# A fused attention and two dense layers: q and k turned by VectorE, reciprocal sums spread by DMA, one threshold per block, two rotating PSUM banks

## The chip, the cores and the metric

The kernel runs on one core of a Trainium2 chip. The metric is the device time of one execution in microseconds (us), as the median of several runs. TensorE (PE in the profile, PEld for its weight loads), VectorE (DVE), ScalarE (ACT) and GpSimd (POOL) have one instruction queue each and work through it in order. SyncE (SP) has the queue from which nearly all DMAs of this kernel are issued.

## The reference

```python
q, k, v: [4, 8, 576, 64]; tau: 0.02; moe_w_in, moe2_w_in: [512, 2048]; moe_w_out, moe2_w_out: [2048, 512]

scores = (1 / 8) * q @ k^T                          # per batch and head, 576 x 576
scores = where(scores >= max(scores, -1) - tau, scores, -1e9)
attn = exp(scores - max(scores, -1)); attn = attn / (sum(attn, -1) + 1e-9)
x = (attn @ v), heads side by side                  # 2304 tokens x 512
h = x @ moe_w_in;  g = where(h >= 1, h, where(h <= -1, 0, (h + 1)^2 / 4));  x = g @ moe_w_out
h = x @ moe2_w_in; g = h * clip(h + 3, 0, 6) / 6;                          out = g @ moe2_w_out
```

All inputs and the output are float32.

## The kernel before

**Jobs and blocks.** Attention is cut into 16 jobs, one for each batch and pair of heads, and a job into five blocks of query rows (four of 128 rows for both heads, and one that holds the 64 remaining rows of both heads). A step of the loop in `attention()` emits the score products of one block and the later stages of earlier blocks. For a block: `em_scores` multiplies `qt` and `kt` (both with the head's 64 dimensions on the partitions) into a pair of PSUM banks P0/P1 (L296); VectorE copies the negated scores to SBUF and takes their extreme (L309); `em_exp` runs the exponential on ScalarE (L320) and adds tau to the extreme on VectorE (L322, once for each of the block's two halves); `em_mask` masks and sums on VectorE (L328); `em_pt` and `em_tail` turn the masked block with TensorE against the identity (`turn`, L254) and ScalarE copies the result to SBUF (L352, L366); `pv_chunk` multiplies with v (L388), and ScalarE copies the result to `xu` (L394).

**q and k.** Both are loaded with rows on the partitions (`load_q`, `load_k`), and `unit_q` and `unit_k` turn them with five and six TensorE transposes (L254, tiles `qn` and `kn`) into a P pair, which ScalarE copies to `qt` (L266, scaling q) and `kt` (L277). The unit of job j+1 is emitted in the last steps of job j.

**The sums.** `pre_norm` takes the reciprocals of a job's nine columns of sums; GpSimd spreads each over 64 columns (L412). Some steps later `em_norm` turns them with TensorE (four transposes at L426 and one at L429, into a P pair) and VectorE multiplies `xu` by the result (L431, L437), after which `xu` is written to DRAM (`xd`, L434, L438).

**The first dense layer runs along.** After the fourth job (j = 3) is finished (`ready(0)`), `mode["mlp"]` is set. From then on each `yield` of `attention()` lets 0.57 units of the first dense layer (`dense1`: `em_h`, L633, and `em_part`, L695, over 256 token columns) be emitted into the same queues, and the weights are split into two parts by ScalarE, VectorE and GpSimd (`split_a`, `split_b`: L116 to L139). What is left of that layer after attention is emitted at once, and then the wide dense layers follow (`dense`: L633 and L675).

**PSUM banks.** While the dense layer runs along, all turns of masked blocks go to bank Q0, the product with v to Q1, `em_h` to Q2, and `em_part` accumulates in Q3. P0 and P1 are shared by the scores, the units and the norm.

**Order.** `attention()` has three branches for a step: one before `mode["mlp"]`, one for steps under 35, and one for later steps. A scheduler with a timeline model puts the emitted instructions in order on each engine, within the order that priorities and added dependencies (`after`) allow.

Of the kernel before, what the change touches and what calls it, by code (L numbers as in the profile page):

```python
# [18 lines left out]
def kernel(  # L19
# [27 lines left out]
    NW = len(WIDE)  # L47
    NF1 = 10
    MLAG = 2
    RAW = 3  # L50
# [145 lines left out]
    def zcol(x, c):  # L196
        return 8 if c == NBLK - 1 else c // 2 * 4 + x * 2 + c % 2

    jobs = [(b, hp) for b in range(NB) for hp in range(HP)]
    NJ = len(jobs)  # L200

    att_es = ExitStack()
# [5 lines left out]
    vn = [ap.tile([128, 5, 2, D], F32, name=f"vn{i}") for i in range(2)]  # L208
    qt, kt = {}, {}

    def rows(src):
        return src[0:MAIN, :].rearrange("(p c) d -> p c d", c=4)

    def load_q(j):
        if j >= NJ:
            return
        E = nc.sync if j else nc.scalar
        b, hp = jobs[j]
        for h in HEADS:
            src = q[b, 2 * hp + h]  # L220
            E.dma_start(out=qn[:, 0:4, h * D:(h + 1) * D], in_=rows(src))
            E.dma_start(out=qn[0:TAIL, 4, h * D:(h + 1) * D], in_=src[MAIN:SEQ, :])

    def load_k(j):
        if j >= NJ:
            return
        b, hp = jobs[j]
        for h in HEADS:
            src = k[b, 2 * hp + h]
            nc.sync.dma_start(out=kn[:, 0:4, h * D:(h + 1) * D], in_=rows(src))  # L230
            for r in range(2):
                nc.sync.dma_start(out=kn[r * TAIL:(r + 1) * TAIL, 4, h * D:(h + 1) * D], in_=src[MAIN:SEQ, :])

    def load_v(j):
        if j >= NJ:
            return
        b, hp = jobs[j]
        t = vn[j % 2]
        for h in HEADS:
            src = v[b, 2 * hp + h]  # L240
            nc.sync.dma_start(out=t[:, 0:4, h, :], in_=rows(src))
            nc.sync.dma_start(out=t[h * TAIL:(h + 1) * TAIL, 4, h, :], in_=src[MAIN:SEQ, :])
# [15 lines left out]
    def unit_q(j):  # L258
        if j >= NJ or j in qt:
            return  # L260
        tm = unit_bank().rearrange("p e n -> p (e n)")
        for c in range(5):
            turn(tm[:, c * 128:(c + 1) * 128], qn[:, c, :], c == 0)
        load_q(j + 1)
        qt[j] = ap.tile([128, SEQ], F32, tag="qt", name="qt", bufs=2)
        reads(S.activation(out=qt[j], in_=tm[:, 0:SEQ], func=ACTF.Copy, scale=taus[:, 1:2]))  # L266

    def unit_k(j):

        if j >= NJ or j in kt:  # L270
            return
        tm = unit_bank().rearrange("p e n -> p (e n)")
        for i, c in enumerate((4, 0, 1, 2, 3, 4)):
            turn(tm[:, i * 128:(i + 1) * 128], kn[:, c, :], i == 0)
        load_k(j + 1)
        kt[j] = ap.tile([128, SEQ + TAIL], F32, tag="kt", name="kt", bufs=2)
        reads(S.activation(out=kt[j], in_=tm[:, 128 - TAIL:128 + MAIN + TAIL], func=ACTF.Copy))  # L277
# [37 lines left out]
    def em_exp(j, i, x):  # L315
        p, nm, th, es = blk[j, i]
        if x >= (1 if i == NBLK - 1 else 2):
# [14 lines left out]
    def turned(j, g):  # L332
# [6 lines left out]
        return gt[g, j]  # L339

    def em_pt(j, i, h):

# [15 lines left out]
    def em_tail(j, i):  # L358
# [3 lines left out]
        t = turned(j, g)[1]  # L362
        tl = bank("Q0" if mode["mlp"] else "Q3")
        if i < NBLK - 1:
# [10 lines left out]
    def pv_chunk():  # L375
# [26 lines left out]
    def pre_norm(j):  # L402
        if j not in zt:
            return
        z = zt.pop(j)
        rz = ap.tile([128, 9, 1], F32, tag="rz", name="rz", bufs=2)
        V.tensor_scalar(out=z, in0=z, scalar1=1e-9, scalar2=None, op0=ALU.add)
        V.reciprocal(out=rz[:, :, 0], in_=z)
        rb = ap.tile([128, 4, 2, 64], F32, tag="rb", name="rb")
        for h in HEADS:  # L410
            src = rz[:, 0:8, :].rearrange("p (g h c) o -> p h g c o", g=2, h=2)[:, h]
            G.tensor_scalar(out=rb[:, :, h, :].rearrange("p (g c) n -> p g c n", g=2),  # L412
                            in0=src.to_broadcast([128, 2, 2, 64]),
                            scalar1=1.0, scalar2=0.0, op0=ALU.mult, op1=ALU.add)
        rbs[j] = (rz, rb)

    def em_norm(j):
# [4 lines left out]
        b, hp = jobs[j]  # L422
        rz, rb = rbs.pop(j)
        bm = unit_bank().rearrange("p e n -> p (e n)")
        for c in range(4):
# [16 lines left out]
    def attention():  # L442
# [35 lines left out]
        for t in range(n + 6):  # L478
            mode["t"] += 1
            mode["step"] = True  # L480
            if not mode["mlp"]:
# [9 lines left out]
                for x in now_at("z"):  # L491
                    pre_norm(*x)
                yield
                now = due(1)
# [18 lines left out]
                for x in now_at("n"):  # L513
                    em_norm(*x)
                    yield
            elif t < 35:
                if t < n:
                    em_scores(*order[t])
                    maskq.append(order[t])
                for x in now_at("z"):  # L520
                    pre_norm(*x)
                if t < n:
                    em_exp(*order[t], 0)
                    em_exp(*order[t], 1)
                masked()
                tails(2)
                for x in now_at("q"):
                    unit_q(*x)
                    yield
                for x in now_at("n"):  # L530
                    em_norm(*x)
                    yield
                pv_run(1)
                yield
                now = due(1)
                for x in now_at("k"):
                    unit_k(*x)
                    yield
                for b in now:
                    em_pt(*b, 0)  # L540
                    yield
                pv_run(2)
                for b in now:
                    if b[1] < NBLK - 1:
                        em_pt(*b, 1)
                        yield
                yield
                for b in now:
                    if b[1] in AFTER:
                        pvq.extend((b[0], AFTER[b[1]], c) for c in range(5))  # L550
            else:
# [5 lines left out]
                for x in now_at("z"):  # L557
                    pre_norm(*x)
                masked()
                yield  # L560
# [167 lines left out]
    def fin_out(g, a, i):  # L728
# [7 lines left out]
        if c < nmain:  # L736
            b, r = divmod(c, MAIN // 128)
            nc.sync.dma_start(out=out[b * SEQ:b * SEQ + MAIN, :].rearrange("(p c) d -> c p d", c=4)[r], in_=ob)
        else:
# [265 lines left out]
```

## Time and profile before

| | before |
|---|---|
| three runs, us | 1137.9, 1138.17, 1138.59; median 1138.17 |
| span of the profiled execution, us | 1136.9 (1.27 below the median of the runs) |
| TensorE busy | 1108.0 us, 97% of the span |
| ScalarE busy | 632.6 us, 56% |
| VectorE busy | 575.6 us, 51% |
| GpSimd busy | 404.3 us, 36% |

The span runs from the first to the last instruction of one profiled execution; a run's time also has what lies around it. "Busy" of TensorE is from modelled ends of pipelined matmuls, so two matmuls that overlap are both shown with their whole length: what a matmul takes from the engine is read from the distance of two starts, not from its length. Times in the rows are from the span's start, in us.

### The profile page before, as it was taken

What the parts mean: (1) busy time and instruction counts of PE and PEld (TensorE: products, weight loads), DVE (VectorE), ACT (ScalarE), POOL (GpSimd) and SP (SyncE); (2) the same over time, 40 slices, a digit from 0 to 9 for tenths busy, and PEclk for the clock granted to TensorE, in tenths of its full rate; (3) what the DMA queues carried; (4) which work ended last, traced back from release to release, by engine and by line L of the source; (5) the groups of instructions that cost most, each with busy time, mean ns of one, the idle gap of its engine ahead of it and who ended that gap; (6) DMA issues with size and microseconds to landing.
All of it is one profiled execution on the core that took longest, in us unless ns stands there. A gap on an engine that the chain in (4) does not pass through costs nothing.

```text
span 1136.9 us, 18024 instructions
## 1 busy us (share of the span) xinstructions
PE 1108.0 (97%) x6680; PEld 901.2 (79%) x6680; DVE 575.6 (51%) x1272; ACT 632.6 (56%) x1239; POOL 404.3 (36%) x383
## 2 busy tenths in 40 slices
PE   7998899999999999999999999999999999999998
PEld 5665567778777788788889988888888888898886
DVE  5888887766565565445545756557511111121111
ACT  5787987866666666556566766645432222333222
POOL 0222676411111111136645765557622222222221
PEclk8999999999999999999999999999999999999999
DMA  6434335222111210015322344533110110010001
GB/s 161 106 77 102 109 108 151 63 81 71 47 49 32 53 43 13 11 34 167 98 75 93 117 143 150 184 111 111 38 42 1 32 38 1 10 38 1 19 1 38
DMA packets 105368, 80.09 MB, mean 70 GB/s; under 512 B 66368, under 2 KB 90176, under 8 KB 105280
## 3 DMA queue, kind: packets, MB, share of 16 engines
q1 hardware_dynamic: 103920, 78.64, 23.9%
q8 instruction: 53, 0.87, 0.3%
q10 hardware_dynamic: 1360, 0.30, 0.1%
q14 instruction: 35, 0.29, 0.1%
HBM read 61.60 MB, written 17.30 MB: 69 GB/s over the span
## 4 chain that ended last, share of the span: by engine, by line
PE 88%; ACT 4%; DVE 4%; issue 1%; DMA 1%; POOL 1%; ACTq 0%; SPq 0%; DVEq 0%
PE Q L633 34%; PE P L675 27%; PE Q L695 7%; PE P L296 7%; PE Q L388 6%; PE Q L254 5%; DVE p L309 2%; ACT e L320 1%; PE P L254 1%; DVE p L328 1%; ACT Gf L352 1%; PE P L426 0%; POOL w_c L135 0%; DMA w_raw<-in_moe_w_in_dram 0%; DVE xl L617 0%
## 5 line engine op out<-in xcount | busy, mean ns | idle before, releaser
L651 POOL TENSOR_TENSOR gl<-r,gh 128x512 fp32r<-128x512 f32 (+1 forms) x190 | 203.3, 1071 | 548.4 <-ACT gh L650 547.9
L633 PE MATMUL Q<-xh,wih 128*128 128x512 f32 (+1 forms) x760 | 263.2, 346 | 2.5 <-DVE r L644 2.5
L633 PE MATMUL Q<-xh,wil 128*128 128x512 f32 (+1 forms) x760 | 257.0, 338 | 0.0
L633 PE MATMUL Q<-xl,wih 128*128 128x512 f32 (+1 forms) x760 | 256.8, 338 | 0.0
L647 DVE SCALAR_TENSOR_TENSOR r<-r,Q 128x512 f32<-128x512 f32 (+1 forms) x80 | 50.7, 634 | 249.0 <-ACT r L646 248.9
L650 ACT ACTIVATE gh<-r 128x512 fp32r<-128x512 f32 (+1 forms) x190 | 99.8, 526 | 126.2 <-PE P L675 53.3
L633 PEld LDWEIGHTS Q<-xh,wih 128*128 128x128 f32 x760 | 143.9, 189 | 25.0 <-issue 4.8
L633 PEld LDWEIGHTS Q<-xl,wih 128*128 128x128 f32 x760 | 143.9, 189 | 15.7
L633 PEld LDWEIGHTS Q<-xh,wil 128*128 128x128 f32 x760 | 143.8, 189 | 15.2
L646 ACT ACTIVATE r<-Q,three 128x512 f32<-128x512 f32 (+1 forms) x80 | 51.4, 643 | 143.7 <-PE Q L633 140.6
L309 DVE TENSOR_SCALAR_CACHE_REDUCE p<-P 128x576 f32<-128x576 f32 x144 | 104.3, 754 | 50.2 <-PE Q L254 32.0
L328 DVE SCALAR_TENSOR_TENSOR p<-p,th,e 128x576 f32<-128x576 f32 x144 | 121.3, 860 | 15.7 <-ACT e L320 14.9
L644 DVE SCALAR_TENSOR_TENSOR r<-r,Q 128x256 f32<-128x256 f32 (+1 forms) x110 | 55.0, 500 | 135.1 <-ACT r L643 127.7
L320 ACT ACTIVATE e<-p,nm 128x576 f32<-128x576 f32 x144 | 109.1, 774 | 25.4 <-DVE p L309 24.3
L254 PE MATMUL Q<-ident,p 128*128 128x128 f32 x656 | 109.8, 283 | 11.3 <-ACT Gf L352 4.9
L675 PE MATMUL P<-woh,gh 128*128 128x512 f32 x288 | 112.0, 390 | 0.6 <-DVE ob L733 0.6
L675 PE MATMUL P<-wol,gh 128*128 128x512 f32 x288 | 112.3, 390 | 0.0
L254 PEld LDWEIGHTS Q<-ident,p 128*128 128x128 f32 x656 | 74.5, 141 | 46.3 <-ACT Gf L352 12.7
L675 PE MATMUL P<-woh,gl 128*128 128x512 f32 x288 | 111.0, 390 | 0.0
L296 PE MATMUL P<-kt,qt 64*128 64x288 f32 (+1 forms) x640 | 100.5, 433 | 6.0 <-DVE p L309 4.9
L135 POOL TENSOR_TENSOR w_c<-w_c,w_raw 128x512 int32<-128x512 int32 x64 | 88.6, 1384 | 39.1 <-DVE w_c L133 22.7
L352 ACT ACTIVATE Gf<-Q 128x512 f32<-128x512 f32 x128 | 74.9, 594 | 40.0 <-PE Q L254 39.2
(84 smaller groups left out, 1865.1 us busy)
## 6 DMA issues: line engine op xcount, KB each, us to landing
w_raw<-in_moe_w_in_dram SPq DMA_DIRECT2D x32, 512.0 KB, 4.1
w_raw<-in_moe_w_out_dram SPq DMA_DIRECT2D x32, 512.0 KB, 3.7
kn<-in_k_dram SPq DMA_DIRECT2D x32, 128.0 KB, 2.6
vn<-in_v_dram SPq DMA_DIRECT2D x32, 128.0 KB, 2.9
x2p<-ob SPq DMA_DIRECT2D x16, 256.0 KB, 2.2
x2d<-ob SPq DMA_DIRECT2D x16, 256.0 KB, 4.1
xst<-x2d SPq DMA_DIRECT2D x16, 256.0 KB, 3.3
out_dram<-ob SPq DMA_DIRECT2D x16, 256.0 KB, 2.2
```

The source lines that it names most:

```text
L135: x = G.tensor_tensor(out=c.bitcast(I32), in0=c.bitcast(I32), in1=r, op=ALU.add)
L254: x = T.transpose(out, in_, ident)
L296: mm = T.matmul(o, qt[j][r, c], kt[j][r, k0:k0 + HS], start=True, stop=True, skip_group_check=True)
L309: reads(V.tensor_scalar(out=p[:, x], in0=s[:, :, 0:HS], scalar1=-1.0, scalar2=3e38, op0=ALU.mult, op1=ALU.min, accum_out=nm[:, x:x + 1]), ...
L320: pins["S"] = S.activation(out=e, in_=p[:, x], func=ACTF.Exp, bias=nm[:, x:x + 1], scale=-1.0)
L328: V.scalar_tensor_tensor(out=p[:, x], in0=p[:, x], scalar=th[:, x:x + 1], in1=e, op0=ALU.is_le, op1=ALU.mult, accum_out=zt[j][:, z:z + 1])
L352: S.activation(out=f[:, h, :, d0:d0 + 128], in_=tm.rearrange("p (c n) -> p c n", c=4), func=ACTF.Copy)
L633: mm = T.matmul(h, l[:, kk * 128:(kk + 1) * 128], r, start=(x == 0), stop=(x == 3 * KD - 1))
L650: x = S.activation(out=gh, in_=r, func=ACTF.Copy)
L651: y = G.tensor_tensor(out=gl, in0=r, in1=f32(gh), op=ALU.subtract)
L675: T.matmul(a, l, r, start=(first and x == 0), stop=(last and x == 2))
L695: mm = T.matmul(o, l, r, start=(f == fs[0] and x == 0 and i == 0), stop=(f == fs[-1] and x == 2 and i == 1), skip_group_check=True)
```

## The change

From job five (j = 4; `j >= JT`, 12 of 16 jobs) q and k are loaded in strips, in such a way that each 32x32 square already stands on the partitions where its transpose belongs; one VectorE transpose, which turns 32x32 squares, makes `qt` and `kt`, and GpSimd scales q. In 14 of 16 jobs (`OVER`: all but the fourth and the last) the reciprocals are turned by VectorE as one 128x32 tile, written to DRAM as nine rows, read back one step later with each row repeated on 64 partitions (`fetch_norm`), and GpSimd multiplies `xu` by them. The threshold is one VectorE instruction for both halves of a block. While the dense layer runs along, turns and products with v take two banks in turn (`rotate`). The branch for steps under 35 is gone. From the second batch on, rows of q, k and v are loaded, and rows of the output stored, in natural order.

```diff
+    NAT = 1
+    JT = 4
...
     def zcol(x, c):
-        return 8 if c == NBLK - 1 else c // 2 * 4 + x * 2 + c % 2
+        return 8 if c == NBLK - 1 else x * 4 + c
...
+    OVER = [j for j in range(NJ - 1) if j != HP - 1]
...
+    def strips(t, s0, src, h):
+        n = src.shape[0] // 32
+        flat = t.rearrange("p c n -> p (c n)")
+        for x in range(2):
+            p0 = 64 * h + 32 * x
+            nc.sync.dma_start(out=flat[p0:p0 + 32, 32 * s0:32 * (s0 + n)].rearrange("p (s d) -> p s d", d=32),
+                              in_=src[:, 32 * x:32 * x + 32].rearrange("(s p) d -> p s d", p=32))
...
     def load_q(j):
...
-            E.dma_start(out=qn[:, 0:4, h * D:(h + 1) * D], in_=rows(src))
+            if j >= JT:
+                strips(qn, 0, src, h)
+                continue
+            E.dma_start(out=qn[:, 0:4, h * D:(h + 1) * D], in_=rows(src, b))
...
     def load_k(j):
...
-            nc.sync.dma_start(out=kn[:, 0:4, h * D:(h + 1) * D], in_=rows(src))
+            if j >= JT:
+                strips(kn, 2, src, h)
+                strips(kn, 0, src[MAIN:SEQ, :], h)
+                continue
+            nc.sync.dma_start(out=kn[:, 0:4, h * D:(h + 1) * D], in_=rows(src, b))
...
     def unit_q(j):
...
+        qt[j] = ap.tile([128, SEQ], F32, tag="qt", name="qt", bufs=2)
+        if j >= JT:
+            V.transpose(out=qt[j], in_=qn.rearrange("p c n -> p (c n)")[:, 0:SEQ])
+            load_q(j + 1)
+            G.tensor_scalar(out=qt[j], in0=qt[j], scalar1=taus[:, 1:2], scalar2=None, op0=ALU.mult)
+            return
...
     def unit_k(j):
...
+        kt[j] = ap.tile([128, SEQ + TAIL], F32, tag="kt", name="kt", bufs=2)
+        if j >= JT:
+            V.transpose(out=kt[j], in_=kn.rearrange("p c n -> p (c n)"))
+            load_k(j + 1)
             return
...
     def em_exp(j, i, x):
...
-        V.tensor_scalar(out=th[:, x:x + 1], in0=nm[:, x:x + 1], scalar1=taus[:, 0:1], scalar2=None, op0=ALU.add)
+        if x == n - 1:
+            V.tensor_scalar(out=th[:, 0:n], in0=nm[:, 0:n], scalar1=taus[:, 0:1], scalar2=None, op0=ALU.add)
...
+    def rotate():
+        mode["r"] = 1 - mode.get("r", 0)
+        return bank(f"Q{mode['r']}")
+
     def em_pt(j, i, h):
...
-        tm = bank("Q0" if mode["mlp"] or mode["n"] % 2 else "Q2")
+        tm = rotate() if mode["mlp"] else bank("Q0" if mode["n"] % 2 else "Q2")
...
-        tl = bank("Q0" if mode["mlp"] else "Q3")
+        tl = rotate() if mode["mlp"] else bank("Q3")
...
-            o_t[j, g] = bank("Q1")
+            o_t[j, g] = rotate() if mode["mlp"] else bank("Q1")
...
     def pre_norm(j):
...
+        if j in OVER:
+            V.transpose(out=rq, in_=rp)
+            rd = dram.tile([9, 128], F32, name=f"rd{j}")
+            for a in range(4):
+                nc.sync.dma_start(out=rd[:, 32 * a:32 * a + 32], in_=rq[32 * a:32 * a + 9, :])
+            rbs[j] = (rd, rb)
+            return
...
+    def fetch_norm(j):
+        if j not in rbs or j not in OVER:
+            return
+        rd, rb = rbs[j]
+        for h in HEADS:
+            r = slice(64 * h, 64 * h + 64)
+            nc.sync.dma_start(out=rb[r, 0:MAIN].rearrange("p (c n) -> p c n", c=4),
+                              in_=rd[4 * h:4 * h + 4, :].unsqueeze(0).to_broadcast([64, 4, 128]))
+            nc.sync.dma_start(out=rb[r, MAIN:SEQ], in_=rd[8:9, r].to_broadcast([64, 64]))
...
     def em_norm(j):
...
+        if j in OVER:
+            load_v(j + 2)
+            x = xu.pop(j)
+            G.tensor_tensor(out=x, in0=x, in1=rb, op=ALU.mult)
+            done_jobs.add(j)
+            if b < NB - 1:
+                nc.sync.dma_start(out=xd[b][:, hp, :], in_=x[:, 0:MAIN])
+            nc.sync.dma_start(out=xd[NB][:, hp, b * TAIL:(b + 1) * TAIL], in_=x[:, MAIN:SEQ])
+            return
...
             at(NBLK * j + NBLK + 0, "z", j)
+            at(NBLK * j + NBLK + 1, "f", j)
             at(NBLK * j + NBLK + 4, "n", j)
...
-            elif t < 35:
-                if t < n:
-                    em_scores(*order[t])
-                    maskq.append(order[t])
...
-                tails(2)
...
-                pv_run(1)
...
-                pv_run(2)
...
```

The two branches of `attention()` that remain call `fetch_norm` right after `pre_norm`. The last branch, which now serves all steps with the dense layer, emits the products with v in one go (`pv_run(5)`), where the removed one emitted one, and then two.

## Rows read from the trace of the kernel before

**Rows 1.** Windows: each engine's busy us in four stretches, granted clock, DMA share, GB/s.

```profile
25.00:106.00 81.00, 76.62 (x572) 50.36 (x569) 71.16 (x215) 66.69 (x138) 17.19 (x21) 1.00 0.37 95
106.00:175.00 69.00, 60.08 (x436) 43.27 (x435) 60.67 (x148) 59.52 (x128) 44.92 (x43) 1.00 0.41 116
175.00:486.00 311.00, 305.30 (x2371) 246.19 (x2371) 187.28 (x535) 206.51 (x446) 64.62 (x85) 1.00 0.21 55
486.00:1136.80 650.80, 646.42 (x3194) 547.46 (x3192) 243.27 (x335) 287.68 (x509) 275.98 (x222) 1.00 0.22 67
```

**Rows 2.** The chain that ended last, by line, in 25:106, 106:175 and 175:486.

```profile
by line: PE P L296 27.5%; PE Q L388 20.5%; DVE p L309 11.9%; PE Q L254 11.8%; DVE p L328 6.5%; issue 4.9%; ACT e L320 4.4%; ACT Gf L352 3.6%; ACT qt L266 2.4%; PE P L254 1.7%; ACT kt L277 1.5%; ACT Gt L366 1.4%; DVE th L322 1.3%; DVE xu L43
by line: issue 8.8%; POOL w_c L135 7.4%; PE Q L633 7.1%; ACT e L320 6.5%; DMA w_raw<-in_moe_w_in_dram 6.3%; PE Q L695 5.4%; DVE p L328 5.4%; DVE xl L617 5.4%; DVE p L309 5.2%; PE Q L388 4.3%; ACT w_raw L116 4.3%; PE Q L254 4.2%; DVE w_c L13
by line: PE Q L695 20.3%; PE Q L633 19.4%; PE Q L388 15.3%; PE P L296 14.6%; PE Q L254 14.5%; PE P L254 2.9%; ACT e L320 2.0%; DVE p L309 1.9%; PE P L426 1.5%; issue 1.5%; ACT Gf L352 1.0%; ACT r L642 0.8%; DVE r L644 0.6%; ACT r L643 0.5%;
```

**Rows 3.** Timeline of TensorE at one unit_q, one norm and one unit_k: start, length.

```profile
300.93 0.71 PE L254 MATMUL P<-ident,qn 128*128 128x128 f32 x5
301.57 0.70 PE L296 MATMUL P<-kt,qt 64*64 64x288 f32 x4
...
304.26 0.60 PE L426 MATMUL P<-ident,rb 128*128 128x128 f32 x4
...
304.81 0.49 PE L254 MATMUL Q<-ident,p 128*128 128x128 f32 x3
...
309.30 0.82 PE L254 MATMUL P<-ident,kn 128*128 128x128 f32 x6
309.96 0.60 PE L254 MATMUL Q<-ident,p 128*128 128x128 f32 x4
```

**Rows 4.** The same at two norms where TensorE then stood idle: [idle before <-releaser].

```profile
87.62 0.77 PE L254 MATMUL Q<-ident,p 128*128 128x128 f32 x5 [1.59 <-DVE p L328]
...
206.34 0.66 PE L426 MATMUL P<-ident,rb 128*128 128x128 f32 x4 [1.17 <-ACT qt L266]
```

**Rows 5.** Groups by line of TensorE in 175:486: count, busy us, mean ns.

```profile
L254 PE MATMUL P<-ident,kn 128*128 128x128 f32 x48 | 7.0, 272 | 0.0
L426 PE MATMUL P<-ident,rb 128*128 128x128 f32 x40 | 6.1, 275 | 1.2 <-ACT qt L266 1.2
```

**Rows 6.** Groups by line and shape, whole span: count, busy us, mean ns, idle before.

```profile
L309 DVE TENSOR_SCALAR_CACHE_REDUCE p<-P 128x576 f32<-128x576 f32 x144 | 104.3, 754 | 50.2 <-PE Q L254 32.0 <-PE P L296 17.3
L133 DVE SCALAR_TENSOR_TENSOR w_c<-w_raw,w_c 128x512 uint32<-128x512 uint32 x64 | 72.3, 1130 | 1.6
L139 POOL TENSOR_TENSOR wol<-w_c,woh 128x512 fp32r<-128x512 f32 x32 | 44.7, 1397 | 15.8 <-ACT woh L137 15.7
L322 DVE TENSOR_SCALAR th<-nm,taus 128x1 f32<-128x1 f32 x144 | 25.3, 207 | 0.4
L120 POOL TENSOR_SCALAR w_c<-w_c 128x512 f32<-128x512 f32 x20 | 14.2, 714 | 41.6 <-ACT w_c L119 41.4
L412 POOL TENSOR_SCALAR rb<-rz 128x256 f32<-128x256 f32 x32 | 13.6, 442 | 27.2 <-DVE rz L408 25.2 <-PE Q L633 1.7
L266 ACT ACTIVATE qt<-P,taus 128x576 f32<-128x576 f32 x16 | 11.8, 739 | 1.4 <-PE P L254 1.4
L277 ACT ACTIVATE kt<-P 128x640 f32<-128x640 f32 x16 | 11.2, 703 | 1.1 <-PE P L254 1.0
L431 DVE TENSOR_TENSOR xu<-xu,P 128x512 f32<-128x512 f32 x16 | 11.0, 685 | 16.7 <-PE P L429 10.8 <-ACT xu L394 5.8
L437 DVE TENSOR_TENSOR xu<-xu,P 64x64 f32<-64x64 f32 x32 | 6.9, 215 | 0.2
```

**Rows 7.** Timeline of VectorE at the start of one block in 175:486.

```profile
332.33 0.76 DVE L309 TENSOR_SCALAR_CACHE_REDUCE p<-P 128x576 f32<-128x576 f32 x1 [4.08 <-PE Q L254]
```

**Rows 8.** DMA issues, whole span: queue, count, KB each, median us from issue to landing.

```profile
kn<-in_k_dram SPq DMA_DIRECT2D x32, 128.0 KB, 2.6
```

**Rows 9.** Timeline of SyncE's queue at one load of k: start, length of issue.

```profile
310.71 1.23 SPq L232 DMA_DIRECT2D kn<-in_k_dram  x2
```

More of the change, by code (lines that the diff above doesn't have):

```diff
@@ L209, with rows @@
     qt, kt = {}, {}
-    def rows(src):
-        return src[0:MAIN, :].rearrange("(p c) d -> p c d", c=4)
+    rp = ap.tile([128, 32], F32, name="rp")
+    rq = ap.tile([128, 32], F32, name="rq")
+    G.memset(rp, 0.0)
+    def rows(src, b):
+        if b >= NAT or JT < HP:
+            return src[0:MAIN, :].rearrange("(c p) d -> p c d", c=4)
+        return src[0:MAIN, :].rearrange("(p c) d -> p c d", c=4)
+    def strips(t, s0, src, h):
[5 more added lines that the diff above has]
+                              in_=src[:, 32 * x:32 * x + 32].rearrange("(s p) d -> p s d", p=32))
     def load_q(j):
@@ L240, in load_v @@
             src = v[b, 2 * hp + h]
-            nc.sync.dma_start(out=t[:, 0:4, h, :], in_=rows(src))
+            nc.sync.dma_start(out=t[:, 0:4, h, :], in_=rows(src, b))
             nc.sync.dma_start(out=t[h * TAIL:(h + 1) * TAIL, 4, h, :], in_=src[MAIN:SEQ, :])
@@ L264, in unit_q @@
         load_q(j + 1)
-        qt[j] = ap.tile([128, SEQ], F32, tag="qt", name="qt", bufs=2)
         reads(S.activation(out=qt[j], in_=tm[:, 0:SEQ], func=ACTF.Copy, scale=taus[:, 1:2]))
@@ L275, in unit_k @@
         load_k(j + 1)
-        kt[j] = ap.tile([128, SEQ + TAIL], F32, tag="kt", name="kt", bufs=2)
         reads(S.activation(out=kt[j], in_=tm[:, 128 - TAIL:128 + MAIN + TAIL], func=ACTF.Copy))
@@ L316, in em_exp @@
         p, nm, th, es = blk[j, i]
-        if x >= (1 if i == NBLK - 1 else 2):
+        n = 1 if i == NBLK - 1 else 2
+        if x >= n:
             return
@@ L405, in pre_norm @@
         z = zt.pop(j)
-        rz = ap.tile([128, 9, 1], F32, tag="rz", name="rz", bufs=2)
+        rz = rp[:, 0:9].unsqueeze(2) if j in OVER else ap.tile([128, 9, 1], F32, tag="rz", name="rz", bufs=2)
         V.tensor_scalar(out=z, in0=z, scalar1=1e-9, scalar2=None, op0=ALU.add)
         V.reciprocal(out=rz[:, :, 0], in_=z)
-        rb = ap.tile([128, 4, 2, 64], F32, tag="rb", name="rb")
+        rb = ap.tile([128, SEQ], F32, tag="rb", name="rb")
+        if j in OVER:
[5 more added lines that the diff above has]
+            return
+        rb = rb[:, 0:MAIN].rearrange("p (c h n) -> p c h n", c=4, h=2)
         for h in HEADS:
-            src = rz[:, 0:8, :].rearrange("p (g h c) o -> p h g c o", g=2, h=2)[:, h]
-            G.tensor_scalar(out=rb[:, :, h, :].rearrange("p (g c) n -> p g c n", g=2),
-                            in0=src.to_broadcast([128, 2, 2, 64]),
+            G.tensor_scalar(out=rb[:, :, h, :], in0=rz[:, 4 * h:4 * h + 4, :].to_broadcast([128, 4, 64]),
                             scalar1=1.0, scalar2=0.0, op0=ALU.mult, op1=ALU.add)
         rbs[j] = (rz, rb)
+    def fetch_norm(j):
[7 more added lines that the diff above has]
+            nc.sync.dma_start(out=rb[r, MAIN:SEQ], in_=rd[8:9, r].to_broadcast([64, 64]))
     def em_norm(j):
@@ L423, in em_norm @@
         rz, rb = rbs.pop(j)
+        if j in OVER:
[6 more added lines that the diff above has]
+            nc.sync.dma_start(out=xd[NB][:, hp, b * TAIL:(b + 1) * TAIL], in_=x[:, MAIN:SEQ])
+            return
         bm = unit_bank().rearrange("p e n -> p (e n)")
@@ L492, in attention @@
                     pre_norm(*x)
+                for x in now_at("f"):
+                    fetch_norm(*x)
                 yield
@@ L515, in attention @@
                     yield
-            elif t < 35:
-                if t < n:
-                    em_scores(*order[t])
-                    maskq.append(order[t])
[L520 to L525, printed above, removed]
-                tails(2)
[L527 to L532, printed above, removed]
-                pv_run(1)
[L534 to L541, printed above, removed]
-                pv_run(2)
[L543 to L550, printed above, removed]
             else:
@@ L558, in attention @@
                     pre_norm(*x)
+                for x in now_at("f"):
+                    fetch_norm(*x)
                 masked()
@@ L737, in fin_out @@
             b, r = divmod(c, MAIN // 128)
-            nc.sync.dma_start(out=out[b * SEQ:b * SEQ + MAIN, :].rearrange("(p c) d -> c p d", c=4)[r], in_=ob)
+            if b >= NAT or JT < HP:
+                dst = out[b * SEQ + r * 128:b * SEQ + r * 128 + 128, :]
+            else:
+                dst = out[b * SEQ:b * SEQ + MAIN, :].rearrange("(p c) d -> c p d", c=4)[r]
+            nc.sync.dma_start(out=dst, in_=ob)
         else:
```

## The prediction

> **What bounds the kernel now.** I read the busy time by stretch first [rows 1]. The cuts are the end of the start-up (25), the start of the dense layer beside attention (106), about the step at which the last branch takes over (175), and the end of the turns of masked blocks (486). TensorE is busy 76.6 of 81, 60.1 of 69, 305.3 of 311 and 646.4 of 650.8 us. The granted clock is 1.00 in all four, so no stretch has a clock to win or lose. After 486 nothing of the change runs, and TensorE idles 4.4 us: this part stays as it is. The question is what limits the three stretches before it.
>
> Then I read the chain of waits in each stretch [rows 2]. In 175:486 the five largest entries are all TensorE lines and make 84%; the units (P L254) and the norm (P L426) are in it themselves, with 2.9% and 1.5%. Here TensorE takes its queue without a hole, and work removed from that queue is time. VectorE, ScalarE and GpSimd are busy 60%, 66% and 21% [rows 1], and VectorE waits 4.08 us for TensorE ahead of one block [rows 7]. In 25:106 TensorE lines head the chain too, but VectorE is busy 88% and ScalarE 82%, and their lines make about a third of the chain: TensorE first, with two others close behind. In 106:175 no engine leads: weight splitting on GpSimd, a weight load, ScalarE, VectorE and TensorE take 4 to 9% each, VectorE is busy 88% and ScalarE 86%. That stretch is limited by the sum of chores on those two engines, not by TensorE, which idles 8.9 us.
>
> **TensorE: what leaves its queue.** A unit is priced by the distance from its first start to the next start of something else, since overlapping matmuls are shown with their whole length [rows 3]. unit_q: 301.57 - 300.93 = 0.64 us. A norm: 304.81 - 304.26 = 0.55. unit_k: 309.96 - 309.30 = 0.66. Twelve q units, twelve k units and fourteen norms go. Where they stand: in 175:486 there are 48 turns of kn, six a unit, so 8 units of k, and as many of q; 40 of the norm, four a norm, so 10, of which the last job's stays [rows 5]. That makes 8 x 0.64 + 8 x 0.66 + 9 x 0.55 = 15.4 us, plus the 1.17 us that one norm waited for a P bank which ScalarE was still reading for qt [rows 4]: **16.5 us**. In 25:106 stand the units of jobs j = 4 and 5 and the norms of 0 to 2: 2 x 0.64 + 2 x 0.66 + 3 x 0.55 = 4.3 us. The idle 1.59 us after one of these norms [rows 4] ended with a mask on VectorE, which had the norm's products in its queue; it may go or stay, so 4.3 to 5.9, and I take **4.7**. In 106:175 two units of each kind and two norms make 3.7 us of TensorE, but TensorE doesn't set this stretch; its price comes from the ledger below.
>
> **VectorE: what comes and goes per job.** Gone: four thresholds of 0.207 (five remain of nine), and three products of the norm, 0.685 + 2 x 0.215 = 1.12 us; together 1.94 [rows 6]. New: transposes of 128x576 and 128x640, and a small one of 128x32. No row shows a VectorE transpose. Nearest is a one-input pass over 128x576, 0.754 us at L309; by elements 0.75 and 0.84. The other bound is the slowest pass of the trace, L133 with 1.130 us for 512 columns: 1.27 and 1.41. The small one I put at the 0.207 of L322, from the same rows. So 1.80 to 2.89 us new against 1.94 gone: from -0.1 to +0.95 a job. I take the low end, since a transpose has one input as L309 has. VectorE is then no busier than before, and 175:486, with its 40% of idle time, would hide the high end too.
>
> The Trainium skill ("VectorE: DVE Perf Modes", "The three transpose paths") gives 311 ns for a 128x128 bf16 VectorE transpose, beside 390 ns for TensorE, and says that VectorE turns 32x32 blocks only. By that figure, as an estimate, 576 and 640 columns cost 1.40 and 1.56 us, a little over my high end; VectorE would take about 1.2 us more a job, which for the four jobs turned ahead of 175 would cost up to 5 us of the sum. No row here has a VectorE transpose, so the trace cannot yet decide.
>
> **ScalarE and GpSimd.** ScalarE loses 0.739 + 0.703 = 1.44 us a job and gets nothing. GpSimd loses two spreads of 0.442, and gets the scaling of q, 0.714 x 576/512 = 0.80, and the product on xu, by L139 1.397 x 576/512 = 1.57: +1.49 us a job [rows 6]. At 21% in 175:486 and 65% in 106:175 [rows 1] that lies beside other work. What queues behind it is gl, the low part of the dense layer's activations, which `em_part` uses some f-steps later; without that cover a job would cost 1.5 us, at most 18 in all.
>
> For 106:175, with two jobs: ScalarE -2.9, VectorE -0.3 (up to +1.9), TensorE -3.7. Bounds: +2 us, if VectorE alone sets it, and -3.7; I take **-1.5**, between the two engines that are busiest.
>
> **Moves and transfers.** The units of j+1 keep their place in the step, and the strips are loaded right after the unit that frees the tile, a job ahead of use: about 31 us, as 311 us hold ten norms [rows 1, 5]. A load of k lands in 2.6 us now [rows 8]; even five times that for the finer pieces is 13 us, so nothing waits. SyncE gets ten more DMAs a job (k eight in place of six, eight for the norm), about 0.6 us of issue each [rows 9]: 6 us of 31. What is queued behind the norm's writes and reads is v, xd and weights; the reads wait about 2.6 us for the writes to land. From the reciprocals to `em_norm` are four steps of some 6 us, so rb is there in time. The natural row order moves as many bytes. In 106:175, where a weight load is on the chain with 6.3%, this could cost up to 4 us; at zero elsewhere.
>
> **Rotating banks and the removed branch.** A turn no longer waits for ScalarE to empty Q0. The most this can give is the idle time that is left in 175:486, 311 - 305.3 = 5.7, less the 1.17 already counted, and part of the 8.9 of 106:175 [rows 1]; the least is a loss of the same size in 106:175, if one run of ten products puts off a turn. I take **-1.5**.
>
> **New waits.** q is turned one step ahead. k is the last thing that a job's last step emits, and the scores follow at once; kt now comes out of VectorE's queue, not from TensorE and a 0.70 us copy on ScalarE. Behind the scores waits all of TensorE's queue. With the 4 us holes [rows 7] I take 0.1 us for each of 12 jobs, **+1.2**; bounds 0, and the rival below.
>
> **Sum.** -16.5 - 4.7 - 1.5 - 1.5 + 1.2 = -23.0 us on a span of 1136.9: 1113.9. Runs have a median 1.27 us above that span: 1115.
>
> **Rivals.**
> *More.* The freed ScalarE and the rotating banks also fill the holes of 106:175 and 175:486: another 7 us of the 14.6 idle [rows 1], so 1108. For it: ScalarE has at least 10.8% of the chain in 106:175 (L320, L116) [rows 2]. Against: weight splitting is untouched.
> *About half.* VectorE's transposes cost the high end, SyncE's longer queue delays weights, and the stretches before 175 give nothing or lose 3 us; 175:486 gives back a few waits: -16.5 + 3 + 2.5 = -11, so 1127. For it: 88% and 86% busy in 106:175. The figure of the Trainium skill above would point this way.
> *Slower.* The k transpose stands in VectorE's queue behind the masks of the last block, and the scores of the next job, with TensorE's queue behind them, wait for it. If it waits for an exponential and a mask, priced as L309's pass of 0.754, and for a split of weights (1.13), and then takes its own 0.84 [rows 6], that is 3.5 us for each of 12 jobs, +42: 1138 - 24 + 42 = 1156. It decides from 24/12 = 2.0 us a job. For it: in-order queues, and 88% busy before 175. Against: VectorE's 4 us holes later, and that the transpose waits only for a load that is long there.
> *No change.* The dense layer's share of each `yield` is fixed, so fewer turns could only move idle time from one engine to another; that needs TensorE not to be the limit in 175:486. Against: 98% busy, and 84% of the chain.
>
> **How the numbers follow.** Forecast 0.6 (its own range 1110 to 1121); more 0.13; about half 0.16; slower 0.08; no change 0.03. A measurement of this kernel can tell some 0.2%, 2.3 us. Faster: 0.6 + 0.13 + 0.16 = 0.89; same 0.03; slower 0.08. For the range I leave out the slower case, no change, and the far ends of "more" and "about half": 1105 to 1128. The forecast is 1115.
>
> **What would show it.** Right: the turns of all masked blocks end near 463 rather than 486, and the rest takes 650 us as now; TensorE's idle time up to there is no larger; VectorE's transposes take 0.7 to 0.9 us; no kt or qt among the long waits of TensorE; GpSimd's product near 1.6 us. Wrong: scores (L296's successors) waiting for VectorE's transpose at each job's start; transposes of 1.4 us and more; waits for rb by DMA; or a stretch with the dense layer in which TensorE's idle time grows by what its queue lost.

## The result, and the profile after

The changed kernel takes 1125.43 us (median of four runs, 1124.17 to 1126.53); the kernel before, beside it, 1138.06. The ratio is 0.9896, 95% interval 0.9884 to 0.9908: 12.6 us or 1.0% faster. The forecast was 1115 with a range of 1105 to 1128: the gain is about half of what was forecast.

The busy times of the page of the changed kernel (busy us, share of the span, instructions), whose span is 1124.7 us:

```profile
PE 1086.1 (97%) x6478; PEld 881.8 (78%) x6478; DVE 586.9 (52%) x1204; ACT 614.3 (55%) x1215; POOL 435.5 (39%) x382
```

TensorE lost 21.9 us of busy time, close to the price of the turns that went, but the span lost only 12.2: TensorE's idle time grew from 28.9 to 38.6 us. Where, the windows of the changed kernel tell, in the stretches of [rows 1] with a cut at 474 in place of 486, 3 us behind the last turn of a masked block:

```profile
25.00:106.00 81.00, 70.93 (x488) 43.74 (x487) 66.73 (x180) 58.78 (x123) 21.98 (x17) 0.96 0.50 110
106.00:175.00 69.00, 53.27 (x367) 38.30 (x362) 60.68 (x132) 52.74 (x114) 44.05 (x39) 0.95 0.43 110
175.00:474.00 299.00, 296.35 (x2319) 239.63 (x2317) 200.16 (x518) 202.40 (x451) 91.44 (x89) 1.00 0.27 68
474.00:1124.60 650.60, 646.29 (x3190) 546.67 (x3188) 245.26 (x335) 287.06 (x507) 275.79 (x223) 1.00 0.22 67
```

From 175 on the reading of before holds: TensorE idles 2.7 us of 299. Ahead of 175 it idles 25.8 us where it idled 13.3 [rows 1], and the mean granted clock, 1.00 before, is 0.96 and 0.95. Both stretches did less work in the same time.

The plainest view is the time at which jobs start. The table has, for every kernel of this study, the start of the first pass of VectorE that takes a block's extreme (L309 in the kernel before) in job j, the start of the last turn of a masked block, and the span (us). The names are those of the experiments below.

```
kernel               j=2     j=4     j=6     j=7     j=8    j=12    j=15  last turn    span
before              49.9    89.9   140.1   179.4   216.9   348.8   446.4      485.8  1136.9
after               51.3    92.1   149.7   186.9   221.7   345.1   435.3      471.0  1124.7
e1_norm_late        49.3    90.9   146.1   183.4   218.2   341.5   431.7      467.5  1121.1
e2_turn_late        51.5    94.2   145.7   185.2   226.3   347.6   437.8      473.6  1127.4
e3_branch           52.0    92.8   147.0   187.2   223.6   345.4   435.6      471.3  1125.0
e4_two_thresholds   50.7    90.1   143.5   188.0   222.0   343.4   433.6      469.4  1123.1
c_none              48.9    87.8   138.0   177.4   214.9   346.8   444.5      483.9  1135.1
c_late              48.6    88.6   138.5   179.4   212.5   334.4   424.6      460.4  1114.1
l1_late_newbranch   48.5    88.7   137.5   185.8   220.9   341.6   431.8      467.6  1121.3
l2_late_parts       49.2    89.9   137.9   185.4   219.2   340.7   430.9      466.7  1120.6
f1_fixed_banks      48.2    87.1   137.6   177.4   216.9   342.6   436.1      476.5  1127.5
f2_early_norms      49.9    92.5   140.8   188.7   220.4   342.9   433.1      468.9  1123.9
f3_early_units      48.3    88.6   144.8   187.1   219.4   339.5   429.7      465.5  1119.2
f4_one_threshold    49.4    90.0   139.7   187.9   219.5   339.9   430.1      465.9  1119.6
```

Four of these kernels (before, c_none, c_late, f1_fixed_banks) are all but the same up to about 175, and start job 4 between 87.1 and 89.9 and job 7 between 177.4 and 179.4: one start of one trace is good to 2 or 3 us.

Job 7 of the changed kernel starts 7.5 us later than before, where the forecast had it about 6 us earlier. From there to the last turn it takes 284.1 us against 306.4: 22.3 us gained, more than forecast. Some of that is work put off: behind the last turn stand 19 more matmuls of the dense layer and 2.6 us more, first in the kernel before and then in the changed one:

```profile
485.80:1136.90 651.10, 646.62 (x3196) 547.66 (x3194) 243.27 (x335) 287.88 (x509) 275.98 (x222) 1.00 0.22 67
```

```profile
471.00:1124.70 653.70, 649.29 (x3215) 549.67 (x3213) 245.68 (x336) 289.19 (x514) 276.50 (x223) 1.00 0.22 67
```

All kernels with rotating banks have these 19 matmuls there, and none of the three with fixed banks throughout. So 19.7 us are gained from job 7 to the end, and but for these 2.6 us the loss against the forecast lies ahead of job 7.

**What the new instructions cost.** Groups by line and shape, whole span, of the changed kernel:

```profile
L288 POOL TENSOR_SCALAR qt<-qt,taus 128x576 f32<-128x576 f32 x12 | 21.2, 1763 | 9.8 <-DVE qt L286 8.6 <-PE Q L277 1.1
L481 POOL TENSOR_TENSOR xu<-xu,rb 128x576 f32<-128x576 f32 x14 | 21.0, 1496 | 44.3 <-DMA rb<-rd 12.2 <-ACT Gf L390 10.4 <-DMA qn<-in_q_dram 8.6
...
L356 DVE TENSOR_SCALAR th<-nm,taus 128x2 f32<-128x2 f32 x64 | 18.6, 291 | 1.8
...
L302 DVE STREAM_TRANSPOSE kt<-kn 128x640 f32<-128x640 f32 x12 | 9.7, 808 | 0.0
L286 DVE STREAM_TRANSPOSE qt<-qn 128x576 f32<-128x576 f32 x12 | 9.3, 774 | 1.8 <-DMA qn<-in_q_dram 0.9 <-PE P L328 0.8
...
L356 DVE TENSOR_SCALAR th<-nm,taus 128x1 f32<-128x1 f32 x16 | 3.2, 202 | 0.2
```

The two large transposes cost what the prediction took (0.75 and 0.84 us). GpSimd's scaling of q costs 1.76 us where 0.80 was forecast, its product 1.50 where 1.57 was. And the one threshold for two halves costs 0.291 us in the mean. Added up by length, VectorE saves 144 x 0.207 [rows 6] - 18.6 - 3.2 = 8.0 us of thresholds, where 64 x 0.207 = 13.2 was worked out. By busy time it saves 25.3 - 18.6 - 3.2 = 3.5 us, since the thresholds of before overlap each other: 144 of them are busy for 25.3 us and not 29.8 [rows 6]. As a whole VectorE's busy time rose, from 575.6 to 586.9 us.

**Why some thresholds take over a microsecond.** The timelines of VectorE and of GpSimd in the changed kernel (start, length):

```profile
86.00 1.23 DVE L356 TENSOR_SCALAR th<-nm,taus 128x2 f32<-128x2 f32 x1
...
131.81 0.93 DVE L356 TENSOR_SCALAR th<-nm,taus 128x2 f32<-128x2 f32 x1
```

```profile
85.50 1.70 POOL L141 TENSOR_TENSOR wil<-w_c,wih 128x512 fp32r<-128x512 f32 x1 [2.42 <-ACT wih L139]
...
131.42 1.29 POOL L141 TENSOR_TENSOR wil<-w_c,wih 128x512 fp32r<-128x512 f32 x1
```

Both long ones end within 0.03 us of a GpSimd instruction that began before them: 86.00 + 1.23 = 87.23 beside 87.20, and 132.74 beside 132.71. It is so throughout: in the six kernels with one threshold a block, 52 of those of two columns took over 0.25 us, and all 52 end within 0.04 us of a GpSimd instruction that began before them. Of the 144 thresholds of one column before, none took over 0.215 us, though 24 of them began while a GpSimd instruction ran. The Trainium skill ("SBUF — State Buffer", "Who interferes with whom") says that VectorE's tensor_scalar can enter a mode that takes the port pair shared with GpSimd, and that whoever starts first then keeps it for a whole instruction; these rows agree for two columns, and for one column no run shows such a wait.

**The first norm over DRAM.** From the chain of the changed kernel in 34:47, and then ScalarE's timeline there:

```profile
35.89 4.99 DMA rb<-rd
...
41.05 1.41 POOL xu L481
...
42.48 0.02 ACT xh L649
```

```profile
39.11 0.64 ACT L139 ACTIVATE wih<-w_c 128x512 fp32r<-128x512 f32 x1
42.48 0.42 ACT L649 ACTIVATE xh<-xu 128x256 fp32r<-128x256 f32 x1 [2.73 <-POOL xu L481]
42.80 1.43 ACT L353 ACTIVATE e<-p,nm 128x576 f32<-128x576 f32 x2
```

rb lands 5.0 us after its issue; GpSimd multiplies; and in ScalarE's queue the split of that xu for the dense layer stands ahead of two exponentials of attention, so ScalarE waits 2.73 us and the exponentials with it. The prediction looked at the time until `em_norm` is emitted, and not at where its reader stands in another queue.

**What a gap can cost twice.** Windows of the changed kernel, then TensorE's timeline, and two merged pieces of its chain (the second from 175:474) with the same 20 products:

```profile
90.00:95.00 5.00, 3.20 (x24) 2.20 (x23) 5.00 (x14) 3.63 (x10) 3.01 (x2) 0.98 0.56 91
95.00:100.00 5.00, 5.00 (x27) 2.05 (x24) 4.86 (x14) 2.05 (x3) 1.77 (x2) 0.68 0.60 139
```

```profile
92.34 0.74 PE L277 MATMUL Q<-ident,p 128*128 128x128 f32 x5 [0.68 <-DVE p L362]
94.20 1.79 PE L328 MATMUL P<-kt,qt 64*128 64x288 f32 x8 [1.13 <-DVE p L341]
```

```profile
95.99 3.94 PE Q L426 x20
...
201.71 2.84 PE Q L426 x20
```

VectorE is busy for all of 90:95 and TensorE for 3.20 us; then the granted clock falls to 0.68, a mix of its two levels of 2.4 and 1.2 GHz, and 20 products take 3.94 us where they take 2.84 at 1.00. Over 25:175 the missing clock is 0.04 x 81 + 0.05 x 69 = 6.7 us of TensorE time, the most that it can have cost. A gap does not always bring the lower level: the kernel before had one of 1.59 us in 25:106 [rows 4] and kept 1.00 there [rows 1].

### The profile page after: what moved, and what is told of

It is laid out like the page before. It is cut to its first block, busy times and chain, and to the rows that moved or that the text cites. A ratio compares the mean times of both kernels' runs of the same rounds, so it can differ in the third digit from the quotient of the medians.

```text
span 1124.7 us, 17618 instructions
## 1 busy us (share of the span) xinstructions
PE 1086.1 (97%) x6478; PEld 881.8 (78%) x6478; DVE 586.9 (52%) x1204; ACT 614.3 (55%) x1215; POOL 435.5 (39%) x382
## 4 chain that ended last, share of the span: by engine, by line
PE 86%; DVE 6%; ACT 3%; DMA 2%; issue 1%; POOL 1%; SPq 1%; ACTq 0%; DVEq 0%; POOLq 0%
PE Q L666 35%; PE P L708 28%; PE Q L728 7%; PE P L328 6%; PE Q L426 5%; PE Q L277 5%; DVE p L341 2%; DVE p L362 2%; ACT e L353 1%; DMA qn<-in_q_dram 1%; DMA w_raw<-in_moe_w_in_dram 0%; DMA rb<-rd 0%; DVE w_c L135 0%; ACT Gf L390 0%; SPq L227 0%
## 5 line engine op out<-in xcount | busy, mean ns | idle before, releaser
L362 DVE SCALAR_TENSOR_TENSOR p<-p,th,e 128x576 f32<-128x576 f32 x144 | 123.6, 879 | 15.4 <-ACT e L353 9.6
```

The lines of the kernel that those rows point to most:

```text
L362: V.scalar_tensor_tensor(out=p[:, x], in0=p[:, x], scalar=th[:, x:x + 1], in1=e, op0=ALU.is_le, op1=ALU.mult, accum_out=zt[j][:, z:z + 1])
```

## The experiments

The edits are to the changed kernel. The ratio to the kernel before is from runs on the same chip, with its 95% interval; the changed kernel's own is 0.9896 (0.9884 to 0.9908). Times from different chips are compared by these ratios.

**One part undone at a time.** Norms of jobs 0 to 2 by TensorE (e1_norm_late):

```diff
-    OVER = [j for j in range(NJ - 1) if j != HP - 1]
+    OVER = [j for j in range(NJ - 1) if j >= HP]
```

> The changed kernel with the norms of jobs 0 to 2 by TensorE again (OVER from j = 4 on). Norm theory: in 25:106 of the changed kernel ScalarE's split of xu stood in its queue ahead of exponentials, waiting for GpSimd's product and that for rb from DRAM; undone, the fifth job starts some 5 us earlier and the time is 1118 to 1121. Strip theory: the early loss is the strips' (DMA time, VectorE's turns ahead of 106), so this run stays at 1124 to 1127. Branch theory: the loss lies in 106:175 and comes from the order of the steps, so 1123 to 1126.

1124.39 us, ratio 0.9890 (0.9874 to 0.9907). Job 5 and job 7 come 3.4 and 3.5 us earlier than in the changed kernel, which is the way of the norm theory, but the fifth job (j = 4) comes only 1.2 us earlier where it forecast 5. The ratio is that of the changed kernel within the interval, outside the norm theory's range and inside those of the other two: undone alone, the early norms give nothing.

Jobs 4 to 7 turned by TensorE (e2_turn_late):

```diff
-    JT = 4
+    JT = 8
```

> The changed kernel with q and k of jobs 4 to 7 turned by TensorE again (JT = 8), so strips and VectorE's transposes only in the stretch that TensorE limits. Strip theory: 1117 to 1121, with the loss ahead of 175 gone. Norm theory: 1124 to 1128, since 3.7 + 2.6 us of TensorE work come back and the wait for rb stays. Branch theory: 1125 to 1128.

1128.68 us, ratio 0.9923 (0.9909 to 0.9938): slower than the changed kernel by 0.3%, and job 7 starts at 185.2 all the same. The strip theory falls as a cause by itself, though the loads of q's strips make 9.6% of the changed kernel's chain in 75:106.

The removed branch put back (e3_branch):

```diff
+            elif t < 35:                       # the removed branch, as before
...
-        tm = rotate() if mode["mlp"] else bank("Q0" if mode["n"] % 2 else "Q2")
+        tm = rotate() if mode["t"] > 35 else bank("Q0" if mode["mlp"] or mode["n"] % 2 else "Q2")
```

(the same for the tail and for o; a step before the switch all open products are finished)

> The changed kernel with the removed branch for steps under 35 put back, with fixed banks in those steps and rotating ones after. Branch theory: 106:175 loses 5 us less, 1118 to 1121. Norm and strip theories: within 2 us of 1125.4.

1124.49 us, ratio 0.9892 (0.9876 to 0.9907): nothing. The branch theory falls as a cause by itself.

Two thresholds a block (e4_two_thresholds):

```diff
-        if x == n - 1:
-            V.tensor_scalar(out=th[:, 0:n], in0=nm[:, 0:n], scalar1=taus[:, 0:1], scalar2=None, op0=ALU.add)
+        V.tensor_scalar(out=th[:, x:x + 1], in0=nm[:, x:x + 1], scalar1=taus[:, 0:1], scalar2=None, op0=ALU.add)
```

> The changed kernel with a threshold for each half of a block again (128x1 each, twice). By the prediction's ledger VectorE gets 64 x 0.207 = 13 us more, some 5 of it ahead of 175 where VectorE is busy: 1127 to 1130. Port theory: the 128x2 form takes 0.29 us in the mean and up to 1.23, beside GpSimd's instructions, where the 128x1 form never took over 0.215, so the pair costs little more than the one: 1123 to 1127.

1126.80 us, ratio 0.9911 (0.9896 to 0.9926): 1.4 us more than the changed kernel. The median lies just inside the port theory's range and 0.2 us below the ledger's; the four runs spread over 3.7 us and the interval overlaps that of the changed kernel, so this run does not tell the two apart.

No single part gives the 10 us back. So the next runs went the other way: all parts undone, and then late only.

**All undone, and late only.** The control (c_none): `OVER = []`, `JT = 99`, two thresholds, the old branch, fixed banks.

> Control: the changed file with every part undone that can be undone by itself (units and norms by TensorE in all jobs, two thresholds, the branch for steps under 35, fixed banks); natural row order of the later batches and the order of the nine sum columns stay. If the natural order is free: within 2 us of the kernel before, 1135 to 1139.

1136.47 us, ratio 1.0000 (0.9991 to 1.0010): natural row order and the order of the columns are free.

Late only (c_late):

```diff
-    JT = 4
+    JT = 8
...
-    OVER = [j for j in range(NJ - 1) if j != HP - 1]
+    OVER = [j for j in range(NJ - 1) if j >= 7 and j != HP - 1]
```

and, as above, two thresholds, and the old branch and fixed banks up to step 35:

> Only late: norms over DRAM from j = 7, units by VectorE from j = 8, rotating banks from step 35, old branch before it, two thresholds. Up to step 35 (about 175) this is the kernel before, and after it the changed one. Theory that the change pays only where TensorE limits, and loses ahead of it by VectorE's and GpSimd's new work together (not by one part): the stretch ahead of 175 is as long as before, 175 to the end of the turns is 16 to 19 us shorter, so 1117 to 1121. If the late gain came from the early stretch having put off work, the late gain is smaller here and the time 1122 to 1130.

1114.18 us (1113.31 to 1115.84), ratio 0.9804 (0.9789 to 0.9818): **faster than both kernels**, by 22 us and by 0.9% beyond the changed one, and below the 1117 to 1121 that was expected. Its windows, with a cut at 463, 2.6 us behind the last turn:

```profile
25.00:106.00 81.00, 76.16 (x567) 49.85 (x565) 71.22 (x214) 66.83 (x139) 17.50 (x21) 1.00 0.38 97
106.00:175.00 69.00, 61.28 (x429) 43.79 (x430) 59.79 (x145) 58.05 (x126) 46.40 (x43) 0.98 0.42 112
175.00:463.00 288.00, 287.36 (x2244) 231.45 (x2244) 192.21 (x535) 193.96 (x431) 83.06 (x85) 1.00 0.28 68
```

The first two stretches are nearly those of before [rows 1] and job 7 starts at 179.4, as before. The third has lost 23 us, and TensorE idles 0.6 us of 288. As in the changed kernel, 2.6 us of work more stand behind the last turn.

**From late only back towards the changed kernel, one part at a time.** Merged branch and rotating banks from step 24 (l1_late_newbranch):

> As the late-only kernel, with the merged branch and rotating banks from the start of the dense layer (step 24) on. Branch theory: 106:175 is 3 to 6 us longer than in the late-only kernel, 1121 to 1126. If the branch is neutral without the other parts: within 1.5 us of the late-only kernel.

1121.07 us, ratio 0.9863 (0.9847 to 0.9879): 0.59% or 6.7 us lost, nearly all ahead of job 7 (185.8 against 179.4). Windows of the late-only kernel with the merged branch:

```profile
142.00:148.00 6.00, 2.84 (x11) 2.42 (x13) 5.18 (x14) 5.72 (x14) 2.97 (x3) 0.56 0.03 11
148.00:154.00 6.00, 5.71 (x27) 4.52 (x23) 5.61 (x9) 2.07 (x6) 3.49 (x3) 0.58 0.13 26
```

The same of the late-only kernel:

```profile
142.00:148.00 6.00, 4.95 (x34) 4.36 (x33) 5.37 (x12) 4.30 (x12) 5.00 (x5) 0.88 0.00 0
148.00:154.00 6.00, 6.00 (x44) 3.95 (x43) 5.07 (x17) 5.42 (x13) 3.72 (x4) 1.00 0.42 107
```

38 matmuls in these 12 us against 78, at 0.56 and 0.58 of the clock against 0.88 and 1.00, with VectorE and ScalarE busy for 5.18 and 5.72 of 6 us in the first window. With one threshold as well (l2_late_parts):

> As the one with the merged branch, with one threshold a block everywhere (so it is the changed kernel with early norms and early units undone at once). Ledger of the prediction: 13 us less of VectorE, some 4 ahead of 175, so 1 to 4 us faster than the same with two thresholds. Port theory: one 128x2 threshold, which can wait for a GpSimd instruction, saves little: within 1.5 us. Theory of interplay: early norms and early units each cost, and undone together they give 4 us or more against the changed kernel, though each alone gave 1 and -3.

1124.91 us (1122.41 to 1126.06; the profiled execution had a span of 1120.6), ratio 0.9900 (0.9883 to 0.9916): slower than with two thresholds by 0.37%, with intervals that do not overlap. The ledger had it faster and the port theory within 1.5 us, so both fail. And early norms and early units undone together, with the merged branch kept, leave the changed kernel's time as it was: the theory of that interplay falls too.

The late-only kernel with fixed banks in all steps (f1_fixed_banks):

> The late-only kernel (1114.2 us, ratio 0.980) with fixed banks in all steps: Q0 for turns, Q1 for the product with v. If the late gain beyond the 16 us of removed turns is the rotating banks': the idle time of TensorE in 175:486 comes back, 3 to 5 us, 1117 to 1120. If the idle time went with the norm's and the units' use of the P banks: within 1.5 us of 1114.

1130.15 us, ratio 0.9932 (0.9918 to 0.9947): 1.3%, some 14.6 us, lost against the late-only kernel, and none of it ahead of job 7 (177.4). This is the largest single number of the study, far beyond both guesses. Window of this kernel, then the waits of TensorE's weight loads and matmuls in 175:463 (us in total, times, longest), and the same waits of the kernel before in 175:486:

```profile
175.00:463.00 288.00, 279.04 (x2121) 219.16 (x2122) 189.81 (x532) 187.57 (x414) 82.22 (x78) 0.99 0.27 66
```

```profile
PEld Q L277 <- ACT Gf L389: 8.2, 23, 1.5
...
PEld P L328 <- DVE p L341: 5.2, 11, 0.7
...
PE Q L277 <- ACT Gf L389: 3.9, 7, 1.3
PE P L328 <- DVE p L341: 2.9, 10, 0.5
```

```profile
PEld Q L254 <- ACT Gf L352: 3.6, 12, 0.5
...
PE Q L254 <- ACT Gf L352: 1.0, 3, 0.3
```

With the same turns gone, TensorE idles 9.0 us of 288 where it idles 0.6 with rotating banks, and gets through 2121 matmuls where it got through 2244. Of the engines, it waits most for ScalarE to empty Q0, 8.2 and 3.9 us where the kernel before has 3.6 and 1.0, and then for VectorE to take the scores out of P, 5.2 and 2.9 us. From job 8's start to the last turn: 268.9 us before, 259.6 with turns gone and fixed banks, 248.0 with both. To the end of the kernel, which takes in the work put off: 920.0, 910.6 and 901.6 us.

The late-only kernel with early norms (f2_early_norms, `OVER` as in the changed kernel):

> The late-only kernel with the norms of jobs 0 to 2 and 4 to 6 over DRAM too. Norm theory (ScalarE's split of xu stands ahead of exponentials and waits for GpSimd's product and rb): 2 to 4 us lost in 25:106, and more in 106:175, so 1117 to 1121. If only the interplay with the strips' DMAs made rb late: within 1.5 us of 1114.

1125.39 us, ratio 0.9886 (0.9871 to 0.9900): 9.3 us lost, more than expected; by job 4, before any strip is turned, this trace is 3.9 us behind that of the late-only kernel. ScalarE's wait for GpSimd's product is there without strips. Waits in 25:106, which the late-only kernel doesn't have:

```profile
POOL xu L480 <- DMA rb<-rd: 21.1, 2, 11.2
...
ACT xh L687 <- POOL xu L480: 4.9, 3, 2.7
```

With early units (f3_early_units, `JT = 4`):

> The late-only kernel with q and k of jobs 4 to 7 from strips by VectorE too. If VectorE's turns cost where VectorE is busy (four jobs, 1.6 us of VectorE and 1.7 of GpSimd each): 1117 to 1121. By the prediction's ledger (VectorE is second, TensorE loses 5.2 us): 1110 to 1114.

1119.75 us, ratio 0.9841 (0.9826 to 0.9855): 4.2 us lost, although 5 us of TensorE work went. Waits of ScalarE for VectorE in 106:190, first of this kernel, then of the late-only one:

```profile
ACT e L353 <- DVE p L341: 5.4, 5, 3.1
```

```profile
ACT e L353 <- DVE p L341: 0.4, 1, 0.4
```

With one threshold a block (f4_one_threshold):

> The late-only kernel with one threshold a block. Prediction's ledger: 5 us less VectorE ahead of 175, 1 to 3 us faster, 1111 to 1113. Port theory: the 128x2 form waits for GpSimd's instruction, so nothing is saved where GpSimd is busy: 1113 to 1116, with 128x2 at 0.25 to 0.3 us in the mean against 0.205.

1121.86 us, ratio 0.9862 (0.9845 to 0.9878): 6.6 us *lost*; neither theory had it. In 106:190 its thresholds and masks, and then the masks of the late-only kernel:

```profile
L362 DVE SCALAR_TENSOR_TENSOR p<-p,th,e 128x576 f32<-128x576 f32 x20 | 22.9, 1163 | 2.2 <-ACT e L353 1.7
...
L356 DVE TENSOR_SCALAR th<-nm,taus 128x2 f32<-128x2 f32 x9 | 3.4, 380 | 0.2
```

```profile
L361 DVE SCALAR_TENSOR_TENSOR p<-p,th,e 128x576 f32<-128x576 f32 x20 | 20.2, 1028 | 3.4 <-ACT e L353 3.3
```

The two-column form takes 0.380 us in this stretch, and 20 masks 2.7 us more. What made the masks longer, and by what path 6.6 us were lost, is not shown. It is not the clock: the mean granted clock is 1.00 in 25:106 and 0.98 in 106:175, as in the late-only kernel.

## Why the prediction was right or wrong

**What bounds the kernel: right, but for the clock.** 175:486 is TensorE's, and late only is where all of the gain is. "No stretch has a clock to win or lose" failed: ahead of 175 the granted clock fell to 0.96 and 0.95, worth 6.7 us at most. How much of the loss that is, and whether TensorE's shorter queue brought it, is not shown.

**TensorE's ledger: right as busy time, not as time.** 21.9 us of busy time went, where 15.4 + 4.3 + 3.7 = 23.4 was worked out. "Work removed from that queue is time" held only together with the rotating banks: with fixed banks (f1_fixed_banks), taking away 8 x 0.64 + 8 x 0.66 + 8 x 0.55 = 14.8 us gave a ratio of 0.9932, or 7.7 us.

**VectorE's ledger: the transposes right, the threshold mis-sized.** 0.774 and 0.808 us, beside 0.75 and 0.84. The 1.40 and 1.56 us worked out from the Trainium skill's transpose figure ("VectorE: DVE Perf Modes", "The three transpose paths") are about twice what the trace shows; the measurement decides. The thresholds gave 3.5 us of busy time where 13.2 was worked out, and no time that the runs can tell: two thresholds, put back, moved the time by 1.4 us with overlapping intervals, and one threshold, put into the late-only kernel, cost 6.6. The prediction read the 0.207 of a row as the price of each, though the row's 25.3 us for 144 show that they overlap, and it priced the new form by the old one, though the new one can wait for GpSimd. "No busier than before" failed as well: VectorE is busy for 11.3 us more.

**GpSimd: mis-sized.** Scaling q took 1.76 us, not 0.80. From 175 on it cost nothing that shows, as TensorE idles 2.7 us of 299.

**25:106, forecast -4.7: failed.** Job 4 starts 2.2 us later. One start is good to 2 or 3 us only, but the traces agree: the five kernels with the norms of jobs 0 to 2 over DRAM start job 4 at 90.1 to 94.2, the nine others at 87.1 to 90.9. "rb is there in time" looked at when `em_norm` is emitted; the split of xu stood earlier in ScalarE's queue. So one of the prediction's own signs of being wrong, waits for rb by DMA, came about.

**106:175, forecast -1.5 between -3.7 and +2: failed, beyond its bounds.** From job 4 to job 7 it takes 94.8 us where it took 89.5. The bound of +2 us was a sum of busy times; what came was idle time: TensorE idles 15.7 us in 106:175 where it idled 8.9, more than the 3.7 that its queue lost, which the prediction had named as another sign of being wrong. VectorE is as busy there as before, ScalarE is not (76% for 86%). Each part alone, put into the late-only kernel, cost more than any ledger: merged branch with its rotating banks 6.7, norms 9.3, units 4.2, one threshold 6.6 us. They don't add: all together cost 10.5. The merged branch and one threshold together (l2_late_parts) already cost 10.9. So one part is enough to lose a good share and this pair to lose all of it, which fits that undoing one of the four gave nothing.

**Rotating banks, forecast -1.5: mis-sized by ten times.** The bound, "the idle time that is left in 175:486", was that of the kernel before. With the turns of q, k and the norm gone and the banks fixed, the waits for Q0 grew from 3.6 and 1.0 us to 8.2 and 3.9. The likely reading is that these turns had covered them. From job 8 to the end, turns gone gave 9.4 us without rotation and 18.4 with it; rotating banks with the turns in place were not run, so that the two need each other is not shown.

**New waits at the job's start: right.** In the changed kernel no wait of TensorE for kt or qt shows from 80 to 474, so the +1.2 was too much. The slower rival did not come about.

**The sum.** Late: -16.5 - 1.5 + 1.2 = -16.8 forecast, -22.3 measured from job 7 to the last turn and +2.6 behind it. Early: -6.2 forecast, +7.5 measured. That 1125 lies within 1105 to 1128 is in part luck: early stretches that came out 13.7 us worse than forecast were partly made up for by a late gain that was mis-sized the other way. The forecast's own range of 1110 to 1121 was missed. "About half", 1127, is the rival that the result is nearest to; it named the stretches ahead of 175, but not what went wrong there: the transposes were not slow, and the weights' loads make 7.4% of the chain in 106:175 where they made 6.3% [rows 2].

**Open.** How much of the loss in 106:175 is the port that VectorE and GpSimd share, and how much the order that the scheduler's model made, was not separated. Rotating banks without the removed turns were not tried, nor, of the pairs of early parts, any but the merged branch with one threshold. The executions of one experiment lie 1 us (the control) to 3.9 us apart, so differences of 1 or 2 us between kernels say nothing.

## What to carry to other kernels

Put a change that unloads one engine only where that engine limits, stretch by stretch: here the same edits gave 22 us late and took 10 back early. A bound taken from today's idle time didn't hold for two edits made together (14.6 us came where 5.7 were idle): ask what covers a wait now, and whether the other edit takes that cover away. When a result moves behind a DMA, look for its first reader in every engine's queue, not for the line that emits it.

## What the runs showed of the hardware that was not expected

A VectorE threshold of two columns took up to 1.23 us when it ended with a GpSimd instruction, one of one column never over 0.216 in any kernel of this study. GpSimd's product of a 128x576 tile with a column from SBUF took 1.76 us, more than its product of two 128x576 tiles with 1.50. Near gaps in TensorE's work the granted clock stood at 0.56 to 0.68 in stretches of 5 and 6 us; the kernel before, which has a gap of 1.59 us in 25:106 [rows 4], kept 1.00 there.
